# Attention outputs normalised on chip before they are stored: a fused Fourier-mixing and multi-query-attention kernel

## The chip, the cores and the metric

The kernel runs on one core of one Trainium2 chip. The metric is device time in microseconds (us), lower is better. Three runs of the kernel before gave 1739.33, 1739.38 and 1740.87 us, a median of 1739.38 us. Engines are named as the profile names them: PE is TensorE (PEld its weight loads), DVE is VectorE, ACT is ScalarE, POOL is GpSimd, SP is SyncE, which here only issues DMAs.

## The reference

```python
def _A_ref(x, dft_seq_re, dft_seq_im, dft_hid_re, dft_hid_im):
    a = jnp.einsum("bsd,ed->bse", x, dft_hid_re)
    b = jnp.einsum("bsd,ed->bse", x, dft_hid_im)
    return jnp.einsum("ts,bse->bte", dft_seq_re, a) - jnp.einsum("ts,bse->bte", dft_seq_im, b)

def _B_ref(x, wq, wk, wv, wo):          # B, S, D = 1, 2048, 640; H = 32 heads of Dh = 20
    q = (x @ wq).reshape(B, S, H, Dh).transpose(0, 2, 1, 3)
    k = x @ wk                          # one key head and one value head for all
    v = x @ wv
    p = _softmax(jnp.einsum("bhqd,bkd->bhqk", q, k) * (Dh ** -0.5), axis=-1)
    o = jnp.einsum("bhqk,bkd->bhqd", p, v)
    return o.transpose(0, 2, 1, 3).reshape(B, S, H * Dh) @ wo

g = _sigmoid((x * gate_w).sum(-1, keepdims=True))
out = g * _A_ref(x, ...) + (1 - g) * _B_ref(x, ...)
```

All arrays are float32. The change concerns the division by the softmax's sums, between `p @ v` and `@ wo`.

## The kernel before

**Stages.** The first 220 us or so compute queries, keys, values, the gate and the hidden-dimension transform. Then, up to about 1560 us, one long hand-ordered stage interleaves four streams on PE, by a string `PLAN` with one letter per step: `a` matmuls (scores whose row maximum is taken), `b` matmuls (the same scores transposed, from which the probabilities come), `av` matmuls (probabilities times values) and `y` matmuls (the sequence transform). Scores of `a` are reduced by DVE (`mx<-a`, line 363), scores of `b` are exponentiated by ACT (`pt<-b`, line 831). Both kinds share six PSUM banks, so a score matmul waits until DVE or ACT has emptied the bank that it is to write. From about 1560 to 1663 us the last pair's `b` and `av` work runs beside the last `y` products in a loop of 16 rounds (lines 1035 to 1052). Then comes the output projection: 32 groups (`o_group`) of 15 matmuls.

**Heads go in 16 pairs**, each in two halves of 1024 queries (qh = 0, 1). A half's attention output and its softmax sums come out of one PSUM bank, 32 rows for each of two heads times two blocks of 512 queries: 20 rows of output and, in row 20, the sum. `finish_half` (line 847) copies the bank to an SBUF tile `ob` (two buffers, so that a half takes the buffer of the same half of the pair before).

**Sums.** For pairs 0 to 14, once both halves are done, the sums are read back from DRAM as 128 x 32 (`sm`), inverted by DVE 24 ticks later (`finish_sums`), stored (`rec_d`) and spread, by a DMA from DRAM to DRAM, over the 20 rows of each head (`rx_d`). The last pair does the same for each half by itself, 4 ticks later. The projection loads 256 columns of outputs and 256 columns of spread reciprocals (`load_o`), POOL multiplies them (`mult_o`, line 628), DVE splits the product into a high and a low part (`split_o`, lines 644 and 645) and PE multiplies these by the weights.

**What sets the order.** PE, ACT, DVE and POOL execute in the order in which the program is written; `later(n, f)` puts f into it n ticks later, and `tick()` is called once for every two score matmuls. SP's order is not written by hand: the scheduler of the programming layer sets it from the dependences, and SP then issues its DMAs strictly in that order, each after its own waits. `move` (line 118) issues all of them, so line 118 is the line of every DMA. SP goes round eight completion semaphores, and a DMA waits for the one issued eight before it where the program does not yet know that to be done.

Of the kernel before, what the change touches and what calls it, by code (L numbers as in the profile page):

```python
# [8 lines left out]
F32 = mybir.dt.float32  # L9
F32R = mybir.dt.float32r  # L10
AF = mybir.ActivationFunctionType
ALU = mybir.AluOpType
# [5 lines left out]
P = 128  # L18
S = 2048
D = 640  # L20
H = 32
DH = 20
KC = D // P
NT = S // P
NPAIR = H // 2
LAST = NPAIR - 1
# [3 lines left out]
ROW = 512  # L30
# [4 lines left out]
def kernel(  # L35
# [13 lines left out]
    nc = tc.nc  # L49
    ctx.enter_context(tc.manual_schedule(engines={ET.PE, ET.Activation, ET.DVE, ET.Pool}))  # L50

    dram = ctx.enter_context(tc.tile_pool(name="dram", bufs=1, space=DRAM))
# [28 lines left out]
    oT_d = dram.tile([D, S], F32, name="oT_d")  # L81
    m_d = dram.tile([NPAIR, P, 2, 32], F32, name="m_d")
    sum_d = dram.tile([H, S], F32, name="sum_d")
    rec_d = dram.tile([H, S], F32, name="rec_d")
    rx_d = dram.tile([D, S], F32, name="rx_d")
    y_d = dram.tile([S, D], F32, name="y_d")


# [25 lines left out]
    def words(ap):  # L114
        return ap.bitcast(F32) if ap.dtype == F32R else ap

    def move(dst, src, queue=nc.sync):
        queue.dma_start(words(dst), words(src))
# [210 lines left out]
    abp = ctx.enter_context(tc.tile_pool(name="abp", bufs=1))  # L329
# [62 lines left out]
    def later(n, f, *args):  # L392
        todo.append((clock["n"] + n, f, args))

    def tick():
        clock["n"] += 1
        due = [t for t in todo if t[0] <= clock["n"]]
        todo[:] = [t for t in todo if t[0] > clock["n"]]
        for _, f, args in due:
            f(*args)  # L400
# [138 lines left out]
    for t in range(NT):  # L539
# [4 lines left out]
        for i in range(2):  # L544
# [4 lines left out]
            for e in range(2):  # L549
                ps = [rot(f"ab_{t}_{i}_{e}_{g}")[:, :HALF] for g in range(2)]  # L550
                es = slice(e * HALF, (e + 1) * HALF)
                for c in range(KC):
                    mm3_rows(ps, xh[:, c], xl[:, c], wh[i][:, c, es], wl[i][:, c, es], KC, c)
                    n = KC * (4 * (t - 2) + 2 * i + e) + c + 1
# [29 lines left out]
    op = ctx.enter_context(tc.tile_pool(name="op", bufs=2))  # L584


    TW = 2 * P
    wos, oraw, ospl, yrow = {}, {}, {}, {}
# [18 lines left out]
            wos[c] = split_w  # L607

    oT_v = oT_d.rearrange("(c p) t -> p c t", p=P)
    rx_v = rx_d.rearrange("(c p) t -> p c t", p=P)  # L610
    NO = S // TW

    def load_o(n):

        if n < NO:
            oraw[n] = []
            for k, v in enumerate((oT_v, rx_v)):
                if (n % 2, k) == (1, 1):
                    t = op.tile([P, KC, TW], F32, name="oraw", bufs=1)
                else:  # L620
                    t = abp.tile([P, KC, TW], F32, tag=f"ab{5 + 2 * (n % 2) + k}0", name="oraw")
                move(t, v[:, :, n * TW : (n + 1) * TW])
                oraw[n].append(t)

    def mult_o(n):
        if n < NO:
            o, r = oraw[n]
            nc.gpsimd.tensor_tensor(o, o, r, op=ALU.mult)  # L628

    def split_o(n):  # L630
        if n < NO:
            if n % 4 == 0:

                h, l = [
                    qbuf[(LAST + 1 + k) % 3][:, : KC * TW].rearrange("p (c t) -> p c t", c=KC)
                    for k in range(2)
                ]
            else:
                h, l = [
                    abp.tile([P, KC, TW], F32R, tag=f"ab{2 * (n % 4 - 1) + k}1", name="osp")  # L640
                    for k in range(2)
                ]
            o = oraw.pop(n)[0]
            nc.vector.tensor_copy(h, o)
            nc.vector.tensor_tensor(l, o, h.bitcast(F32), op=ALU.subtract)
            ospl[n] = (h, l)

    def load_y(tb):
        if tb < NT:
            yrow[tb] = spare(tb, "yrow")  # L650
            move(yrow[tb], y_d[tb * P : (tb + 1) * P])

    def gate_y(tb):
        if tb < NT:
            nc.scalar.activation(yrow[tb], yrow[tb], AF.Copy, scale=gate[:, tb : tb + 1])
# [3 lines left out]
    def o_group(tb, e):  # L659
        n, k = divmod(tb, 2)  # L660
        es, tk = slice(e * HALF, (e + 1) * HALF), slice(k * P, (k + 1) * P)
        rows = slice(tb * P, (tb + 1) * P)
        ps = orot(f"o_{tb}_{e}")[:, :HALF]
        h, l = ospl[n]
        for c in range(KC):
            mm3(ps, h[:, c, tk], l[:, c, tk], wos[c][0][:, es], wos[c][1][:, es], KC, c)
        oy = op.tile([P, HALF], F32, tag=("yt", "yu")[e], name="oy")
        nc.vector.scalar_tensor_tensor(
            oy, ps, omg[:, tb : tb + 1], yrow[tb][:, es], op0=ALU.mult, op1=ALU.add
        )  # L670
        move(out[rows, es], oy)
# [165 lines left out]
    def av_step(p, qh, kc):  # L837
        if kc == 0:
            av[qh] = bank("V", f"av_{p}_{qh}")
        for hh in range(2):  # L840
            for j in range(2):
                t, slot = pt.pop((hh, kc, 2 * qh + j))
                known["PE"] = max(known["PE"], slot[0])
                av_mm(av[qh], 2 * hh + j, t, kc, kc == 0, kc == NT - 1)
                ptfree.append(slot)

    def finish_half(p, qh):
        ob = op.tile([P, ROW], F32, name="ob")
        nc.scalar.activation(ob, av[qh], AF.Copy)
        for hh in range(2):  # L850
            h = 2 * p + hh
            for j in range(2):
                js = slice((2 * qh + j) * ROW, (2 * qh + j + 1) * ROW)
                g = 32 * (2 * hh + j)
                move(sum_d[h : h + 1, js], ob[g + DH : g + DH + 1])
                move(oT_d[h * DH : (h + 1) * DH, js], ob[g : g + DH])
        if p == LAST:
            sm = op.tile([P, 16], F32, name="sm")
            ts = slice(qh * S // 2, (qh + 1) * S // 2)
            for hh in range(2):  # L860
                move(sm[64 * hh : 64 * hh + 64], sum_d[2 * p + hh, ts].rearrange("(s t) -> s t", t=16))
            later(4, finish_last, ts, sm)
        elif qh == 1:
            sm = op.tile([P, 32], F32, name="sm")
            move(sm, sum_d[2 * p : 2 * p + 2].rearrange("h (s t) -> (h s) t", t=32))
            later(24, finish_sums, p, sm)

    def finish_sums(p, sm):
        rc = op.tile([P, 32], F32, name="rc")
        nc.vector.reciprocal(rc, sm)  # L870
        move(rec_d[2 * p : 2 * p + 2].rearrange("h (s t) -> (h s) t", t=32), rc)
        for hh in range(2):
            h = 2 * p + hh
            move(
                rx_d[h * DH : (h + 1) * DH], rec_d[h : h + 1].to_broadcast([DH, S])
            )

    def finish_last(ts, sm):

        rc = op.tile([P, 16], F32, name="rc")  # L880
        nc.vector.reciprocal(rc, sm)
        for hh in range(2):
            h = 2 * LAST + hh
            move(rec_d[h, ts].rearrange("(s t) -> s t", t=16), rc[64 * hh : 64 * hh + 64])
            move(rx_d[h * DH : (h + 1) * DH, ts], rec_d[h : h + 1, ts].to_broadcast([DH, S // 2]))

    SCORES = "abcdefABCDEFghijklGHIJKL"
    PLAN = (
# [94 lines left out]
    BEFORE = {  # L988
        **{kk: (lambda c=kk - 1: load_wo((c,)),) for kk in range(1, 1 + KC)},
        12: (lambda: load_o(0), lambda: load_o(1)),  # L990
        13: (lambda: mult_o(0), lambda: mult_o(1)),
        14: (lambda: split_o(0), lambda: load_o(2)),
        15: (lambda: [load_y(tb) for tb in range(4)],),
    }
# [10 lines left out]
    def next_v():  # L1005
        st = taken["V"] - LAG
        taken["V"] += 1
        if st >= 0:
            av_step(*STEPS[st])
            if STEPS[st][2] == NT - 1:  # L1010
                finish_half(*STEPS[st][:2])

    for what in PLAN:
# [7 lines left out]
        else:  # L1021
            kind, s = divmod(SCORES.index(what), 6)
# [31 lines left out]
    for _ in range(2):  # L1054
        y_evict()
    split_o(1)
    load_o(3)


    gate_y(0)  # L1060
    for i in range(2 * NT):
        tb, e = divmod(i, 2)
        if e == 0:
            gate_y(tb + 1)
        o_group(tb, e)
        tick()
        if i == 0:
            for st in old:
                av_step(*st)
            finish_half(*old[-1][:2])  # L1070
        n, k = divmod(i, 4)
        if k == 1:
            mult_o(n + 2)
        elif k == 2:
            split_o(n + 2)
            load_o(n + 3 if n else NO)
        if e == 1:
            load_y(tb + 4)
# [47 lines left out]
```

## Time and profile before

| | |
|---|---|
| median of three runs | 1739.38 us |
| the profiled execution | 1738.29 us |
| its span (first to last instruction) | 1736.5 us |
| PE busy | 1725.9 us (99%) |
| DVE busy | 1433.4 us (83%) |
| ACT busy | 1195.2 us (69%) |
| POOL busy | 817.0 us (47%) |
| TensorE clock granted | 1.0 |

A row of the timeline reads: start in us from the span's start, duration in us, engine and line, operation, out<-in, shapes, how many instructions were merged, and in brackets the idle time of that engine just before, with what ended it. SPq rows are DMA issues: what they show is the time that SP spends on the issue, not the transfer. A row of a group reads: busy us and mean ns of one, then the idle time of the engine in front of such instructions and what ended most of it.

### The profile page before, as it was taken

To read this page: it belongs to the slowest core of one execution; us is meant where nothing else is said; L and a number is where in the kernel's file an instruction comes from. 1 tells how busy PE (TensorE), PEld (TensorE's weight loads), DVE (VectorE), ACT (ScalarE), POOL (GpSimd) and SP (SyncE) were. 2 spreads that over 40 slices of the span, in tenths; PEclk is the share of its full clock that TensorE was granted. 3 is DMA by queue.
4 is the path that set the end of the run, shared out by engine and by line. 5 is a ranking of instruction groups with operands and counts; after the bars stand their busy time and mean duration, and the time that the engine had idled before them with its cause. 6 is when DMAs were issued, how large, how long until landed. Compare 5 with 4: busy or idle time off the path is not lost.

```text
span 1736.5 us, 40769 instructions
## 1 busy us (share of the span) xinstructions
PE 1725.9 (99%) x16342; PEld 1214.6 (70%) x16342; DVE 1433.4 (83%) x2355; ACT 1195.2 (69%) x2337; POOL 817.0 (47%) x559
## 2 busy tenths in 40 slices
PE   9999999999999999999999999999999999999998
PEld 8899976666666666666666666666666666667788
DVE  5779998989888898888898889888888898855254
ACT  4722257777777777777777777777777777777731
POOL 1012153563645463756656565565654344542242
PEclk9999999999999999999999999999999999999999
DMA  8873433333344443435453444343443242325667
GB/s 289 242 210 99 129 117 100 121 125 101 121 136 131 117 134 104 155 115 163 133 160 115 156 141 129 110 148 106 142 142 115 85 121 90 95 89 177 200 206 250
DMA packets 131002, 243.88 MB, mean 140 GB/s; under 512 B 26356, under 2 KB 77556, under 8 KB 128292
## 3 DMA queue, kind: packets, MB, share of 16 engines
q1 hardware_dynamic: 130012, 238.00, 43.5%
q0 software_dynamic: 800, 3.28, 0.6%
q8 instruction: 128, 2.10, 0.5%
q14 instruction: 62, 0.51, 0.1%
HBM read 194.62 MB, written 50.86 MB: 141 GB/s over the span
## 4 chain that ended last, share of the span: by engine, by line
PE 90%; DMA 3%; issue 3%; POOL 2%; DVE 2%; SPq 0%; ACT 0%; POOLq 0%; DVEq 0%
PE av L835 26%; PE y L694 19%; PE a L356 17%; PE b L821 16%; PE ab L137 7%; PE q L126 1%; PE q L128 1%; PE q L127 1%; DMA oraw<-rx_d 1%; POOL ya L750 1%; POOL oraw L628 1%; DVE mx L363 0%; DMA wraw<-in_wiT_dram 0%; DMA out_dram<-oy 0%; DMA x_d<-both 0%
## 5 line engine op out<-in xcount | busy, mean ns | idle before, releaser
L363 DVE TENSOR_REDUCE mx<-a 128x1 f32<-128x512 f32 x2048 | 1260.1, 681 | 154.9 <-PE a L356 97.3
L831 ACT ACTIVATE pt<-b 128x512 f32<-128x512 f32 x2048 | 1049.5, 619 | 315.0 <-PE b L821 190.6
L694 PE MATMUL y<-x,ch 64*128 64x320 f32 x3584 | 728.3, 304 | 1.1 <-ACT yt L723 1.1
L356 PE MATMUL a<-ks,qs 60*128 60x512 f32 x2048 | 722.0, 414 | 0.3 <-DVE mx L363 0.2
L821 PE MATMUL b<-qs,ks 62*128 62x512 f32 x2048 | 695.0, 414 | 0.3 <-ACT half L566 0.3
L694 PEld LDWEIGHTS y<-x,ch 64*128 64x128 f32 x3584 | 549.9, 186 | 21.6 <-issue 10.5
L694 PE MATMUL y<-x,cl 64*128 64x320 f32 x1792 | 507.6, 304 | 0.0
L835 PE MATMUL av<-pt,vsb 128*32 128x512 f32 x4096 | 502.9, 600 | 0.0
L356 PEld LDWEIGHTS a<-ks,qs 60*128 60x128 f32 x2048 | 350.5, 184 | 139.9 <-DVE mx L363 102.1
L821 PEld LDWEIGHTS b<-qs,ks 62*128 62x128 f32 x2048 | 340.2, 184 | 139.9 <-ACT pt L831 71.0
L694 PEld LDWEIGHTS y<-x,cl 64*128 64x128 f32 x1792 | 309.8, 185 | 3.4 <-issue 2.5
L482 POOL TENSOR_TENSOR craw<-craw 128x1024 f32<-128x1024 f32 x80 | 189.5, 2369 | 254.6 <-DMA craw<-in_cre_dram 117.5
L835 PEld LDWEIGHTS av<-pt,vsb 128*32 128x32 f32 x4096 | 106.2, 108 | 194.3 <-issue 173.5
L493 POOL TENSOR_TENSOR cl<-craw,ch 128x1024 fp32r<-128x1024 f32 x98 | 232.2, 2369 | 7.9
L492 POOL CAST ch<-craw 128x1024 fp32r<-128x1024 f32 x98 | 101.7, 1037 | 149.1 <-PE y L694 120.1
L137 PE MATMUL ab<-wh,xh 64*128 64x320 f32 x640 | 126.6, 297 | 2.3 <-DVE both L567 1.5
L137 PE MATMUL ab<-wl,xh 64*128 64x320 f32 x640 | 126.2, 296 | 0.0
L137 PE MATMUL ab<-wh,xl 64*128 64x320 f32 x640 | 126.1, 296 | 0.0
L750 POOL TENSOR_TENSOR ya<-yt,ya 128x320 f32<-128x320 f32 x64 | 60.7, 965 | 99.3 <-ACT yt L723 98.7
L566 ACT ACTIVATE half<-ab 128x320 f32<-128x320 f32 x64 | 28.0, 437 | 103.9 <-PE ab L137 98.3
L137 PEld LDWEIGHTS ab<-wh,xl 64*128 64x128 f32 x640 | 92.9, 185 | 0.0
L137 PEld LDWEIGHTS ab<-wl,xh 64*128 64x128 f32 x640 | 92.9, 186 | 0.0
(88 smaller groups left out, 1087.6 us busy)
## 6 DMA issues: line engine op xcount, KB each, us to landing
craw<-in_cre_dram SPq DMA_DIRECT2D x96, 512.0 KB
craw<-in_cim_dram SPq DMA_DIRECT2D x96, 512.0 KB
xr<-x_d SPq DMA_DIRECT2D x88, 320.0 KB
qs<-qh_d SPq DMA_DIRECT2D x64, 160.0 KB
x_d<-both SPq DMA_DIRECT2D x64, 160.0 KB
ya<-y_d SPq DMA_DIRECT2D x64, 160.0 KB
y_d<-ya SPq DMA_DIRECT2D x64, 160.0 KB
xr<-in_xT_dram SPq DMA_DIRECT2D x20, 256.0 KB
```

What stands on the lines that cost most here:

```text
L137: nc.tensor.matmul(ps, w[r], woven(x[r]), start=(i == 0 and k == 0), stop=(i == n - 1 and k == 2))
L356: nc.tensor.matmul(ps, qs[p][b : b + 60, qb * P : (qb + 1) * P], woven(ks[b : b + 60, c * ROW : (c + 1) * ROW]), start=True, stop=True,)
L363: return nc.vector.tensor_reduce(mx[p][:, hh, qb, c : c + 1], ps, axis=AX.X, op=ALU.max)
L482: eng.tensor_tensor(raws[0], raws[0], raws.pop(1), op=PRODUCTS[GROUPS[g][0]][0][1])
L492: eng.tensor_copy(h, raw)
L493: eng.tensor_tensor(l, raw, h.bitcast(F32), op=ALU.subtract)
L566: nc.scalar.activation(half, ps[0], AF.Copy, scale=sg)
L694: mm = nc.tensor.matmul(ps[g % len(ps)], w, woven(x), start=start, stop=stop)
L750: nc.gpsimd.tensor_tensor(ya, yt, ya, op=how)
L821: nc.tensor.matmul(ps, ks[b : b + 62, kc * P : (kc + 1) * P], woven(qs[p][b : b + 62, qc * ROW : (qc + 1) * ROW]), start=True, stop=True,)
L831: halves.scored(nc.scalar.activation(t, ps, AF.Exp, scale=SCALE), n)
L835: nc.tensor.matmul(ps[32 * g : 32 * g + 32, :], vsb[:, kc, :], t, start=first, stop=last)
```

## The change

Outputs are no longer stored raw. `finish_half` stores only the sums. For pairs 0 to 14 the sums are read back and inverted 8 ticks later (24 before); the reciprocals are then loaded from DRAM in spread form, each over 32 rows, into two tiles `rb` (eight DMAs of 32 x 512), and 6 ticks after that POOL multiplies the two `ob` tiles by them (two products of 128 x 512) and eight DMAs store the normalised outputs. For each half of the last pair the raw sums are spread by four DMAs into an `rb` tile, and 4 ticks later DVE inverts the whole 128 x 512 tile, multiplies, and four DMAs store. `rx_d`, the loads from it and the eight POOL products of 128 x 1280 in the projection are gone, and a load of outputs has three buffers.

```diff
-    rx_d = dram.tile([D, S], F32, name="rx_d")
...
         if n < NO:
-            oraw[n] = []
-            for k, v in enumerate((oT_v, rx_v)):
-                if (n % 2, k) == (1, 1):
-                    t = op.tile([P, KC, TW], F32, name="oraw", bufs=1)
-                else:
-                    t = abp.tile([P, KC, TW], F32, tag=f"ab{5 + 2 * (n % 2) + k}0", name="oraw")
-                move(t, v[:, :, n * TW : (n + 1) * TW])
-                oraw[n].append(t)
-
-    def mult_o(n):
-        if n < NO:
-            o, r = oraw[n]
-            nc.gpsimd.tensor_tensor(o, o, r, op=ALU.mult)
+            oraw[n] = abp.tile([P, KC, TW], F32, tag=f"ab{5 + n % 3}0", name="oraw")
+            move(oraw[n], oT_v[:, :, n * TW : (n + 1) * TW])
...
+    obs = {}
+
     def finish_half(p, qh):
-        ob = op.tile([P, ROW], F32, name="ob")
+        ob = obs[p, qh] = op.tile([P, ROW], F32, name="ob")
         nc.scalar.activation(ob, av[qh], AF.Copy)
-        for hh in range(2):
-            h = 2 * p + hh
-            for j in range(2):
-                js = slice((2 * qh + j) * ROW, (2 * qh + j + 1) * ROW)
-                g = 32 * (2 * hh + j)
-                move(sum_d[h : h + 1, js], ob[g + DH : g + DH + 1])
-                move(oT_d[h * DH : (h + 1) * DH, js], ob[g : g + DH])
+        for g, h, js in quarters(p, qh):
+            move(sum_d[h : h + 1, js], ob[g + DH : g + DH + 1])
         if p == LAST:
-            sm = op.tile([P, 16], F32, name="sm")
-            ts = slice(qh * S // 2, (qh + 1) * S // 2)
-            for hh in range(2):
-                move(sm[64 * hh : 64 * hh + 64], sum_d[2 * p + hh, ts].rearrange("(s t) -> s t", t=16))
-            later(4, finish_last, ts, sm)
+            rb = spread(sum_d, p, qh)
+            later(4, finish_last, p, qh, rb)
         elif qh == 1:
             sm = op.tile([P, 32], F32, name="sm")
             move(sm, sum_d[2 * p : 2 * p + 2].rearrange("h (s t) -> (h s) t", t=32))
-            later(24, finish_sums, p, sm)
+            later(8, finish_sums, p, sm)
+
+    def quarters(p, qh):
+        for k in range(4):
+            hh, j = divmod(k, 2)
+            yield 32 * k, 2 * p + hh, slice((2 * qh + j) * ROW, (2 * qh + j + 1) * ROW)
+
+    def spread(src, p, qh):
+        rb = op.tile([P, ROW], F32, name="rb")
+        for g, h, js in quarters(p, qh):
+            move(rb[g : g + 32], src[h : h + 1, js].to_broadcast([32, ROW]))
+        return rb
 
     def finish_sums(p, sm):
         rc = op.tile([P, 32], F32, name="rc")
         nc.vector.reciprocal(rc, sm)
         move(rec_d[2 * p : 2 * p + 2].rearrange("h (s t) -> (h s) t", t=32), rc)
-        for hh in range(2):
-            h = 2 * p + hh
-            move(
-                rx_d[h * DH : (h + 1) * DH], rec_d[h : h + 1].to_broadcast([DH, S])
-            )
...
+        rbs = [spread(rec_d, p, qh) for qh in range(2)]
+        later(6, finish_pair, p, rbs)
+
+    def store_o(p, qh):
+        ob = obs.pop((p, qh))
+        for g, h, js in quarters(p, qh):
+            move(oT_d[h * DH : (h + 1) * DH, js], ob[g : g + DH])
+
+    def finish_pair(p, rbs):
+        for qh in range(2):
+            ob = obs[p, qh]
+            nc.gpsimd.tensor_tensor(ob, ob, rbs[qh], op=ALU.mult)
+            store_o(p, qh)
+
+    def finish_last(p, qh, rb):
+        ob = obs[p, qh]
+        nc.vector.reciprocal(rb, rb)
+        nc.vector.tensor_tensor(ob, ob, rb, op=ALU.mult)
+        store_o(p, qh)
...
-        13: (lambda: mult_o(0), lambda: mult_o(1)),
...
-        if k == 1:
-            mult_o(n + 2)
-        elif k == 2:
+        if k == 2:
```

The change moves instructions on two engines at places of which the prediction speaks. On DVE, the inversion of pair 6's sums (pairs count from 0) stands among the maxima of the `a` scores; the first number in a name `a_...` is the score's number. Before:

```order
L363 TENSOR_REDUCE mx_13871<-a_554_1_14842 128x1
L363 TENSOR_REDUCE mx_13871<-a_555_1_14847 128x1
L870 RECIPROCAL rc_14851<-sm_14326 128x32
L363 TENSOR_REDUCE mx_13871<-a_556_1_14856 128x1
L363 TENSOR_REDUCE mx_13871<-a_552_0_14882 128x1
```

and with the change:

```order
L362 TENSOR_REDUCE mx_13926<-a_536_0_14519 128x1
L362 TENSOR_REDUCE mx_13926<-a_537_0_14529 128x1
L862 RECIPROCAL rc_14559<-sm_14377 128x32
L362 TENSOR_REDUCE mx_13926<-a_538_0_14572 128x1
L362 TENSOR_REDUCE mx_13926<-a_538_1_14575 128x1
```

The inversion now stands in front of 32 maxima that stood in front of it.

On SP, the same pair's DMAs from the sums to the reciprocals. Before:

```order
L118 DMA oT_d<-ob 20x512
L118 DMA y_d<-ya 128x320 x2
L118 DMA sm<-sum_d 128x32
L118 DMA ya<-y_d 128x320 x2
L118 DMA craw<-in_cre_dram 128x1024 x2
L118 DMA xr<-x_d_67 128x640
L118 DMA xr<-x_d_68 128x640
```

and with the change:

```order
L117 DMA sum_d<-ob 1x512 x4
L117 DMA y_d<-ya 128x320 x2
L117 DMA ya<-y_d 128x320 x2
L117 DMA sm<-sum_d 128x32
L117 DMA craw<-in_cre_dram 128x1024 x2
L117 DMA rec_d<-rc 128x32
L117 DMA xr<-x_d_67 128x640
L117 DMA xr<-x_d_68 128x640
L117 DMA rb<-rec_d 32x512 x8
L117 DMA oT_d<-ob 20x512 x8
L117 DMA craw<-in_cre_dram 128x1024 x2
```

The load `sm` of the sums still stands behind the two stores of `ya` (a `y` product's update, made by POOL), and now behind two loads `ya` as well; the inversion's store, the spread loads and the outputs' stores stand ahead of the next `craw` loads.

On DVE in the last rounds, where the last pair's first half is inverted between the splits of the transform's blocks (`ch`, `cl`). Before:

```order
L493 TENSOR_TENSOR cl<-craw,ch 128x1024
L881 RECIPROCAL rc<-sm 128x16
L492 CAST ch<-craw 128x1024
L493 TENSOR_TENSOR cl<-craw,ch 128x1024
```

and with the change:

```order
L492 TENSOR_TENSOR cl<-craw,ch 128x1024
L880 RECIPROCAL rb<-rb 128x512
L881 TENSOR_TENSOR ob<-ob,rb 128x512
L491 CAST ch<-craw 128x1024
L492 TENSOR_TENSOR cl<-craw,ch 128x1024
```

The place is the same; a tile of 512 columns is inverted there instead of 16, and a product follows it.

More of the change, by code (lines that the diff above doesn't have):

```diff
@@ L609 @@
     oT_v = oT_d.rearrange("(c p) t -> p c t", p=P)
-    rx_v = rx_d.rearrange("(c p) t -> p c t", p=P)
     NO = S // TW
@@ L642, in split_o @@
                 ]
-            o = oraw.pop(n)[0]
+            o = oraw.pop(n)
             nc.vector.tensor_copy(h, o)
@@ L871, in finish_sums @@
         move(rec_d[2 * p : 2 * p + 2].rearrange("h (s t) -> (h s) t", t=32), rc)
-        for hh in range(2):
-            h = 2 * p + hh
-            move(
-                rx_d[h * DH : (h + 1) * DH], rec_d[h : h + 1].to_broadcast([DH, S])
-            )
[L878 to L885, printed above, removed]
+        rbs = [spread(rec_d, p, qh) for qh in range(2)]
[14 more added lines that the diff above has]
+        store_o(p, qh)
     SCORES = "abcdefABCDEFghijklGHIJKL"
```

## The prediction

> **What bounds the kernel now.** I read the page's first part, then what PE waited for, then the groups of DVE and PE's weight loads.
>
> ```profile
> span 1736.5 us, 40769 instructions
> PE 1725.9 (99%) x16342; PEld 1214.6 (70%) x16342; DVE 1433.4 (83%) x2355; ACT 1195.2 (69%) x2337; POOL 817.0 (47%) x559
> PE o L128 <- DVE osp L645: 0.9, 1, 0.9
> PE o L128 <- DVE qs L645: 0.7, 1, 0.7
> L363 DVE TENSOR_REDUCE mx<-a 128x1 f32<-128x512 f32 x2048 | 1260.1, 681 | 154.9 <-PE a L356 97.3
> L356 PEld LDWEIGHTS a<-ks,qs 60*128 60x128 f32 x2048 | 350.5, 184 | 139.9 <-DVE mx L363 102.1
> ```
>
> PE is idle for 10.6 us in all (1736.5 - 1725.9), so nothing that leaves PE's work as it is can win more than that. Of these the change can reach two waits, 0.9 and 0.7 us, both in the projection, both for a split output. On the other side PE has little cover: DVE's maxima are 1260.1 us of work, and the weight loads of the `a` scores sat 102.1 us behind a maximum that had yet to empty a bank. So in the long stage DVE must not stand still: what it loses there, PE loses soon after.
>
> **The projection: what is removed.** For the last half the reciprocals go through SP and DRAM three times (`rec_d`, `rx_d`, `oraw`) before POOL can multiply. The rows are the timeline's; the last one is of the stretches, for the tile `o` alone (PE's busy time and its matmuls come first):
>
> ```profile
> 1679.31 1.11 SPq L118 DMA_DIRECT2D rec_d<-rc  x2
> 1686.89 1.10 SPq L118 DMA_DIRECT2D oraw<-rx_d  x1
> 1694.01 2.91 POOL L628 TENSOR_TENSOR oraw<-oraw 128x1280 f32<-128x1280 f32 x1 [19.14 <-DMA oraw<-rx_d]
> 1696.95 0.83 DVE L644 CAST qs<-oraw 128x1280 fp32r<-128x1280 f32 x1 [7.42 <-POOL oraw L628]
> 1699.36 0.40 PE L128 MATMUL o<-wo,qs 128*128 128x320 f32 x1 [0.68 <-DVE qs L645]
> 1664.00:1736.50 72.50, 65.76 (x479) 64.79 (x477) 16.25 (x32) 1.00 0.72 231
> ```
>
> PE stands 0.68 us until the split's low part is there at 1699.3; it wanted it at 1698.7. The second wait, two windows of 256 columns later, has the same form (POOL's product, then the split) and 0.9 us. With the change the way is: sums stored, spread, inverted, multiplied, outputs stored, loaded, split. What is new in it is DVE's work, priced by these groups:
>
> ```profile
> L870 DVE RECIPROCAL rc<-sm 128x32 f32<-128x32 f32 x15 | 5.1, 341 | 0.0
> L881 DVE RECIPROCAL rc<-sm 128x16 f32<-128x16 f32 x2 | 0.5, 253 | 10.6 <-DMA sm<-sum_d 10.6
> L520 POOL TENSOR_TENSOR xr<-xr 128x640 f32<-128x640 f32 x40 | 62.2, 1556 | 0.0
> ```
>
> 16 columns more cost the inversion 88 ns, 5.5 ns each, so 512 columns cost 0.25 + 496 x 0.0055 = 2.98 us (should the slope not hold, not below a product's time); the product half of the 1.23 that a subtraction of 1024 columns takes (row 1629.84 below), with overhead 0.7; together 3.7. The inversion before stood just ahead of the `rec_d` row, near 1678. From there: 3.7, four stores issued and landed 3.3 (issues of 0.25, row 863.77, and 2.2 for a landing, row 1628.50, both below), a load of outputs 7.1 (1686.89 to 1694.01 is one, with issue), the cast 0.83 and the subtraction 1.5: 1694.4. So the first wait goes, with 4 us to spare, and the later windows, which no longer load a second tile nor pass POOL, lose theirs: **-1.7 us** with the restarts (bounds: 0, and 2). DVE's 3.7 us hold up outputs behind them, but an output group of 15 matmuls takes PE 15 x 65.76 / 479 = 2.1 us and seven banks take turns.
>
> **The long stage: the inversion that moves.** Pairs 0 to 14 invert 8 ticks after their second half instead of 24. Pair 6:
>
> ```profile
> 861.33 0.62 ACT L849 ACTIVATE ob<-av 128x512 f32<-128x512 f32 x1
> 863.77 0.25 SPq L118 DMA_DIRECT2D sum_d<-ob  x1
> 871.64 1.70 POOL L750 TENSOR_TENSOR ya<-yt,ya 128x320 f32<-128x320 f32 x2 [3.96 <-ACT yt L723]
> 871.92 7.99 DVE L363 TENSOR_REDUCE mx<-a 128x1 f32<-128x512 f32 x13 [0.41 <-PE a L356]
> 872.53 1.17 SPq L118 DMA_DIRECT2D y_d<-ya  x2
> 873.81 0.37 SPq L118 DMA_DIRECT2D sm<-sum_d  x1
> 874.23 0.92 SPq L118 DMA_DIRECT2D ya<-y_d  x2
> 893.15 0.34 DVE L870 RECIPROCAL rc<-sm 128x32 f32<-128x32 f32 x1
> ```
>
> 24 ticks took 893.15 - 861.33 = 31.8 us, so 8 take 10.6 and the inversion's new place is at 871.9, just where the run of 13 maxima starts (the order: 32 places earlier, at about 0.6 us each). But SP, which issues in its order, had stored the sums by 864 and then stood behind `y_d<-ya` until POOL gave the `ya` at 872.5; only then came `sm`, at 873.81. In the new order two `ya` loads stand ahead of `sm` too: 872.53 + 1.17 + 0.92 + some gaps = 874.7. How long such a load takes to land, the last pair's first half shows:
>
> ```profile
> 1626.31 0.50 SPq L118 DMA_DIRECT2D sm<-sum_d  x1
> 1628.50 0.25 DVE L881 RECIPROCAL rc<-sm 128x16 f32<-128x16 f32 x1 [10.57 <-DMA sm<-sum_d]
> 1629.84 1.23 DVE L493 TENSOR_TENSOR cl<-craw,ch 128x1024 fp32r<-128x1024 f32 x1
> 1633.29 0.30 PE L694 MATMUL y<-x,ch 64*128 64x320 f32 x2
> ```
>
> 2.2 us, with DVE waiting for nothing else. So pair 6's sums are in SBUF at 876.9 and DVE stands still from 871.9: **5.0 us**. Behind the inversion on DVE stand the 13 maxima, and PE waits for their banks. It has an `av` run and a spare bank or two in hand, which I put at 0.5 us, since the 13 maxima are back to back and the delay passes to the last of them. PE loses **4.5 us** (bounds 3.5 and 5). That cannot be made up: the matmuls behind are the same and PE was never idle there.
>
> Pair 4 is the second such place, for another reason: two 512 KB `craw` loads are issued just ahead of the sums' stores, and these come down behind them.
>
> ```profile
> 684.60 0.60 ACT L849 ACTIVATE ob<-av 128x512 f32<-128x512 f32 x1 [0.24 <-PE av L835]
> 689.49 0.42 SPq L118 DMA_DIRECT2D craw<-in_cim_dram  x1
> 690.80 0.21 SPq L118 DMA_DIRECT2D sum_d<-ob  x1
> 695.10 0.21 SPq L118 DMA_DIRECT2D sum_d<-ob  x1
> 697.29 0.35 SPq L118 DMA_DIRECT2D sm<-sum_d  x1
> 717.95 0.34 DVE L870 RECIPROCAL rc<-sm 128x32 f32<-128x32 f32 x1
> ```
>
> A third of 717.95 - 684.60 is 11.1: the new place is 695.7. The four stores of sums no longer alternate with the outputs' stores, so the last is issued near 692 instead of 695.1; `sm` follows when they have landed. If nothing were in their way, `sm` at 694 and no wait; if the loads hold them as before, `sm` at 697.3, in SBUF at 699.5, and a wait of 3.8. The loads are the same, so I take the middle, 1.9, less 0.2 of cover: **1.7 us**. Pair 9 has two such loads ahead of it and its reckoning ends even:
>
> ```profile
> 1130.39 0.60 ACT L849 ACTIVATE ob<-av 128x512 f32<-128x512 f32 x1
> 1141.46 0.34 SPq L118 DMA_DIRECT2D sm<-sum_d  x1
> ```
>
> (new place near 1141.5, and `sm` not much earlier than 1141). For it and its like (in pairs 5, 7 and 8 too a large load or a wait for POOL stands just ahead of `sm`) I take **0.5 us** together; bounds 0, and 2 each. In the other pairs the new place leaves more room.
>
> **The long stage: what is added.** Per pair two POOL products of 128 x 512, 1556 x 512/640 = 1.25 us each, 37 us in all; and on SP 26 DMAs in place of 20, with `craw` loads behind outputs' stores that wait for POOL. Both are covered by POOL's lead:
>
> ```profile
> L482 POOL TENSOR_TENSOR craw<-craw 128x1024 f32<-128x1024 f32 x80 | 189.5, 2369 | 254.6 <-DMA craw<-in_cre_dram 117.5
> L492 POOL CAST ch<-craw 128x1024 fp32r<-128x1024 f32 x98 | 101.7, 1037 | 149.1 <-PE y L694 120.1
> ```
>
> POOL waited 120.1 us for PE to give a `ch` buffer back, which only an engine that is ahead does. Such a lead is half a group of `y` matmuls or more, over 10 us by the count of steps, and a pair's late loads take up to 10 of it and have 80 us to give it back. I cost this at nothing; without the lead each late microsecond of a `cl` would be one of PE's. ACT's next copy into an `ob` comes half a pair, some 45 us, after the inversion, and finds the outputs stored.
>
> **The last rounds.** At 1628.50 DVE waits for the first half's sums; behind stands a split whose `cl` ended at 1629.84 + 1.23 = 1631.1, wanted by PE at 1633.3 by count of the steps (the last row). 3.7 instead of 0.25 us would end it at 1634.5, 1.2 late; but the spread loads follow the sums' stores at once and come about 1.5 earlier than the second `sm` did. I take **0.3 us** (bounds 0 and 1.5).
>
> **Sum:** -1.7 + 4.5 + 1.7 + 0.5 + 0.3 = +5.3. The profiled execution took 1738.29 us, its span 1736.5 and 1.8 around it; with the change span 1741.8 and 1743.6. The median before is 1.1 above the profiled execution: **1744.7 us**.
>
> **Rivals.**
> (1) *The sums come in time.* `sm` lands before DVE reaches the inversion, or DVE's idle share (154.9 us before the maxima) swallows the wait. For it: four DMAs fewer stand ahead of `sm`. Against it: in pair 6 SP stands behind POOL, whatever its list. Then the projection's gain is left, 1739.4 - 1.7 = 1737.7; with half of pair 6's wait, 1739.9. 0.25.
> (2) *SP becomes the brake* (slower). SP stands at the outputs' stores until POOL has multiplied, `craw` is late by more than POOL's lead, and PE waits at the next `cl`. It decides from a delay of about 12 us in a pair; at 5 us in one pair of three it adds 25 to the waits above: some 1765; in one or two pairs, 1752. For it: `rb` and stores are 16 DMAs in a row. Against it: the 120.1 us. 0.11.
> (3) *POOL's products hold DVE up* (slower). Here these rows:
>
> ```profile
> 861.91 4.87 DVE L363 TENSOR_REDUCE mx<-a 128x1 f32<-128x512 f32 x8 [0.18 <-PE a L356]
> 867.24 4.28 DVE L363 TENSOR_REDUCE mx<-a 128x1 f32<-128x512 f32 x7 [0.45 <-PE y L694]
> 1657.95 3.52 DVE L644 CAST qs<-oraw 128x1280 fp32r<-128x1280 f32 x1 [3.64 <-POOL oraw L628]
> ```
>
> The cast took 3.52 us at 1657.95, beside a POOL product, and 0.83 at 1696.95, alone. If 30 products held a maximum each for their 1.25 us, 37 us: 1777. Against it: 8 maxima took 0.609 us each while POOL worked, 7 took 0.611 while it mostly waited. 0.01. [...]
> (4) *More goes than the two waits*, by a traffic without `rx_d` that feeds the long stage earlier: PE waits for no DMA there, so little can be won; 1734. 0.03.
>
> **How the numbers follow.** The forecast has 0.60, and by the bounds of its terms its own range is 1741 to 1748. A difference of 0.2% (3.5 us, about what a measurement of this kernel can tell) puts 1742.9 as the edge of slower: 0.51 of the 0.60 lies above it, with (2) and (3) 0.63. Of (1) 0.21 is within, with 0.09 of the forecast 0.30. Faster is below 1735.9: the rest of (1) and (4), 0.07. The range that leaves out 2 in 10 reaches down into (1), 1738, and up past the forecast's own, 1750.
>
> **What would show it.** Right: DVE's inversions (group `rc<-sm`) with idle time ahead of them ended by the DMA `sm<-sum_d`, near 5 us in one and 2 to 3 in another, and PE idle on maxima in the long stage, where it has none now; no wait of `o` for `osp` or `qs`; an inversion of 512 columns near 3 us. Wrong: no idle time ahead of `rc` (then rival 1), or PE waiting at `y` for `cl` (rival 2), or maxima longer than 681 ns (rival 3).

## The result, and the profile after

The changed kernel takes **1762.47 us** (median of 4 runs, 1757.29 to 1764.73) where the kernel before, run beside it, takes 1739.39: a ratio of 1.0126, 95% interval 1.0102 to 1.0151. Forecast were 1744.7 and a range of 1738 to 1750. The direction was right, the size was not: 23 us slower, not 5.

Of the changed kernel, the span, the busy times and three groups of DVE:

```profile
span 1762.4 us, 40890 instructions
...
PE 1737.7 (99%) x16342; PEld 1222.9 (69%) x16342; DVE 1436.6 (82%) x2357; ACT 1196.4 (68%) x2337; POOL 829.1 (47%) x581
...
L362 DVE TENSOR_REDUCE mx<-a 128x1 f32<-128x512 f32 x2048 | 1260.7, 681 | 158.6 <-PE a L355 98.8
...
L880 DVE RECIPROCAL rb<-rb 128x512 f32<-128x512 f32 x2 | 6.7, 3346 | 9.5 <-DMA rb<-sum_d 9.5
L862 DVE RECIPROCAL rc<-sm 128x32 f32<-128x32 f32 x15 | 5.2, 346 | 14.3 <-DMA sm<-sum_d 14.3
```

Two things differ. PE is idle for 24.7 us (1762.4 - 1737.7) where it was for 10.6. And the same 16342 matmuls now keep it busy for 11.8 us more. The maxima take 681 ns as before, so POOL's products do not hold DVE up. The inversions `rc<-sm` now have 14.3 us of DVE's idle time ahead of them, ended by the load of the sums; before they had none. What PE waited for (us in total, times, longest):

```profile
PE a L355 <- DVE mx L362: 8.0, 4, 4.2
PE b L808 <- DVE mx L362: 3.2, 2, 2.7
PE ab L136 <- DVE both L566: 2.7, 1, 2.7
...
PE b L808 <- DMA qs<-m_d: 1.0, 1, 1.0
PE y L681 <- DVE cl L492: 0.7, 1, 0.7
```

The waits of `o` for `osp` and `qs` are gone, as forecast; 11.2 us of waits for maxima have come, in the long stage, where there were 0.2. The timeline at pair 6, on SP:

```profile
872.22 1.11 SPq L117 DMA_DIRECT2D sum_d<-ob  x4
882.78 1.17 SPq L117 DMA_DIRECT2D y_d<-ya  x2
884.00 0.92 SPq L117 DMA_DIRECT2D ya<-y_d  x2
885.08 0.32 SPq L117 DMA_DIRECT2D sm<-sum_d  x1
```

on DVE:

```profile
877.48 4.27 DVE L362 TENSOR_REDUCE mx<-a 128x1 f32<-128x512 f32 x7 [0.47 <-PE y L681]
887.82 0.35 DVE L862 RECIPROCAL rc<-sm 128x32 f32<-128x32 f32 x1 [6.06 <-DMA sm<-sum_d]
```

and on PE:

```profile
884.12 0.48 PE L808 MATMUL b<-qs,ks 62*128 62x512 f32 x1
888.77 0.79 PE L355 MATMUL a<-ks,qs 60*128 60x512 f32 x1 [4.16 <-DVE mx L362]
```

The stores of the sums are issued by 873.3, SP then stands until POOL has given `ya` at 882.8, `sm` follows at 885.1, DVE stands 6.06 us and PE 4.16. But PE's first matmul behind the stop takes 0.79 us, where an `a` takes 0.41 on the mean. The stretches around it show why (a row has, after the length: busy time of PE, PEld, DVE, ACT and POOL with their instructions, the granted clock, the DMA share, GB/s):

```profile
881.30:884.70 3.40, 3.31 (x27) 1.14 (x23) 0.45 (x1) 1.65 (x5) 1.70 (x2) 1.00 0.20 73
884.70:888.13 3.43, 0.00 (x0) 0.00 (x0) 0.32 (x2) 0.54 (x1) 0.00 (x0) 1.00 0.77 237
888.13:891.54 3.41, 2.77 (x15) 2.68 (x17) 3.41 (x7) 1.20 (x2) 0.64 (x1) 0.50 0.99 354
891.54:894.96 3.42, 3.42 (x24) 3.42 (x23) 2.67 (x5) 2.28 (x4) 3.27 (x3) 0.50 0.70 163
894.96:898.40 3.44, 3.44 (x34) 1.66 (x34) 2.97 (x6) 2.64 (x5) 3.44 (x3) 1.00 0.10 31
```

From 888.13 to 894.96 the granted clock is 0.50: two stretches of 3.41 us, in each of which a busy PE gets through 1.7 us less work (an estimate, 0.50 x 3.41). In all traces of this case the lowest clock is 0.50, and by the clock's records it stays there for 3.413 us (in the first profile of the changed kernel at 103.06, 1164.61 and 1591.27) or twice that (6.827 at 888.13; longer at one place of experiment 4, where PE stood for 13.6 us; what follows the last matmul is left out). A stop here therefore cost its length and then 0, 1.7 or 3.4 us.

Where the time came from, by the delay of ACT's instructions against the same instructions in the first trace of the kernel before (the median over 20 us, read behind each place), for the first profile of the changed kernel and for a second one taken later (experiment 6):

| place | forecast | first profile | second profile |
|---|---|---|---|
| first 100 us, untouched by the change | none | +5.4 | +0.3 |
| pair 4 | +1.7 | +2.9 | +4.9 |
| pair 6 | +4.5 | +7.1 | +6.0 |
| pairs 5, 7, 8 and 9 | +0.5 | +7.0 | +5.0 |
| a load of `qs` that SP issues late (near 860) | none | +1.4 | +1.2 |
| the rest of the long stage | none | +0.4 | +0.7 |
| half clock behind PE's 1.1 us wait for `yt`, a wait that was there before too | none | +1.7 | +1.7 |
| last rounds | +0.3 | +1.6 | +1.4 |
| projection | -1.7 | -1.6 | -1.5 |
| sum (differences of the spans: 25.9 and 19.6) | +5.3 | +25.9 | +19.7 |

Without the first row, which is not the change's doing (experiment 7), the two profiles are 20.5 and 19.4 us late.

### The profile page after: what moved, and what is told of

Its sections match the earlier page's. It is cut to its first block, busy times and chain, and to the rows that moved or that the text cites. A ratio compares the mean times of both kernels' runs of the same rounds, so it can differ in the third digit from the quotient of the medians.

```text
span 1762.4 us, 40890 instructions
## 1 busy us (share of the span) xinstructions
PE 1737.7 (99%) x16342; PEld 1222.9 (69%) x16342; DVE 1436.6 (82%) x2357; ACT 1196.4 (68%) x2337; POOL 829.1 (47%) x581
## 4 chain that ended last, share of the span: by engine, by line
PE 88%; DMA 4%; POOL 4%; DVE 1%; issue 1%; SPq 1%; ACT 1%; POOLq 0%; DVEq 0%
PE av L822 25%; PE y L681 19%; PE b L808 15%; PE a L355 15%; PE ab L136 7%; PE o L125 1%; PE o L126 1%; PE o L127 1%; PE q L125 1%; PE q L126 1%; DMA craw<-in_cim_dram 1%; PE q L127 1%; POOL cl L492 1%; POOL craw L481 1%; DMA sm<-sum_d 1%; DVE mx L362 1%
```

## The experiments

Theory W (waits and clock): DVE's waits for the sums stop PE, and the stops bring stretches at half clock. Theory T (traffic): the products on POOL, the added DMAs and SP's order cost the time.

**1. 14 ticks.**

```
-            later(8, finish_sums, p, sm)
+            later(14, finish_sums, p, sm)
```

> The changed kernel with one number altered: the inversion of pairs 0 to 14 is called 14 ticks after the half instead of 8 (18.6 us instead of 10.6). Theory W (waits and clock): the changed kernel loses its time where DVE stands at an inversion whose sums are not yet loaded, PE stops behind it, and the granted clock falls for some us after the longer stops. Against the trace of before, ACT's copies are later by 2.9 us behind pair 4, 0.7 behind pair 5, 7.1 behind pair 6, 1.3, 0.9 and 4.2 behind pairs 7, 8 and 9: 17.1 in all. The latest sums of the changed kernel's trace (pair 6) are loaded 15.6 us after the half's copy, so with 18.6 no inversion waits, and all of the 17.1 go: 1762.5 - 17.1 = 1745.4. What is left above the kernel before is then 5.4 us of delay in the first 100 us, of which W says nothing, and some 2 us of a late load of qs and of the last rounds, less the two waits of the projection. Theory T (traffic): the products on POOL, the six added DMAs per pair and SP's new order cost the time, and the inversion is only where it shows; then 14 ticks move little, and the time stays above 1757.

Measured: 1741.61 us (11 runs, 1740.42 to 1745.03) beside 1739.16 for the kernel before (20 runs, 1736.52 to 1742.94), ratio 1.0016 (1.0007 to 1.0025). From its groups:

```profile
L362 DVE TENSOR_REDUCE mx<-a 128x1 f32<-128x512 f32 x2048 | 1260.4, 681 | 155.5 <-PE a L355 97.7 <-PE b L808 48.1 <-PE y L681 7.8
...
L355 PE MATMUL a<-ks,qs 60*128 60x512 f32 x2048 | 722.6, 414 | 0.4 <-DVE mx L362 0.2
...
L862 DVE RECIPROCAL rc<-sm 128x32 f32<-128x32 f32 x15 | 5.1, 341 | 0.0
```

No inversion waits, PE's idle time ahead of `a` is 0.4 us, and 21 of the 23 us are gone, with all products, DMAs and the new projection kept. T is refuted. The time is 4 us under what W said; W had left the 5.4 us of the first 100 us in its sum (experiment 7 is on these).

**2. The same places without the wait.**

```
-            later(8, finish_sums, p, sm)
+            later(8, finish_sums, p, old_sm.get("sm", sm))
+            old_sm["sm"] = sm
```

> The changed kernel, 8 ticks as it is, but the inversion of pair p reads the loaded sums of pair p-1, which have been in SBUF for 80 us (pair 0 reads its own). All loads and stores, POOL's products and the places of all instructions stay; what is changed in the computation is that the outputs of pairs 1 to 14 are divided by the sums of another pair. W: the inversion never waits, PE is idle for it nowhere, and the 17.1 us of the long stage go: about 1745.4, as with 14 ticks. T: nothing of the traffic is changed, so the time stays above 1757. If the two kernels (this one and the one with 14 ticks) differ by more than 3 us, the place of the inversion costs something else than its wait.

Measured: 1742.37 us (9 runs), ratio 1.0021 (1.0010 to 1.0032), 0.8 us from experiment 1. Its waits of PE, the first lines:

```profile
PE ab L136 <- DVE both L566: 1.4, 1, 1.4
PE warm L267 <- POOL ident masks.py:199: 1.4, 1, 1.4
PE b L808 <- DMA qs<-m_d: 1.3, 1, 1.3
```

So the place 8 ticks after the half costs nothing by itself; the wait there does. What is left of the traffic is the third line: with 8 ticks SP reaches a load of `qs` too late, 1.3 us here and 1.0 in the changed kernel. In experiment 1, with 14 ticks, that wait isn't there (experiment 5, also with 14, has one of 0.4 us at another place).

**3. The moved inversion alone, in the kernel before.**

```
-            later(24, finish_sums, p, sm)
+            later(8, finish_sums, p, sm)
```

> The kernel before with one number altered: the inversion is called 8 ticks after the half instead of 24. No product on POOL, no added DMA; the outputs still go through rx_d. W: in the trace of before the loads of the sums are issued at 697.3, 873.8, 1141.5 and 1320.5 (pairs 4, 6, 9, 11) and land some 2.1 us later; the new places of the inversions are 695.6, 871.9, 1141.9 and 1315.2. DVE stands 3.8, 4.0, 1.7 and 7.4 us, PE some 0.8 less each: 13.7; the clock falls after three of these for 1.5 to 3 us of lost time each: about 7. 1739.4 + 21 = 1760, with waits of PE for mx in the long stage. T: no added traffic, so 1739 to 1741.

Measured: 1756.93 us (4 runs), ratio 1.0095 (1.0078 to 1.0112). Its waits of PE:

```profile
PE a L356 <- DVE mx L363: 6.0, 3, 3.6
PE b L821 <- DVE mx L363: 4.9, 2, 3.8
```

One number moves the kernel before by 17.8 us, without a product or a DMA more. PE stops for 3.6 us at pair 4, 1.1 at pair 5, 2.3 at pair 6 and 3.8 at pair 9. Pair 11 does not wait: in the new order its `sm` is issued 4.0 us behind the half, where it was 13.8. W had counted a wait of 7.4 us there.

**4. Doses.** In the kernel before, 8 ticks after each pair's second half:

```
+            later(8, hold_dve, p)
...
+    dz = op.tile([P, ROW], F32, name="dz", bufs=1)
+    nc.vector.memset(dz, 1.0)
+    def hold_dve(p):
+        for n in ((256,), (384,), (512,), (512, 128), (512, 256))[p % 5]:
+            nc.vector.reciprocal(dz[:, :n], dz[:, :n])
```

> The kernel before, with DVE held up on purpose 8 ticks after each pair's second half by inversions of a scratch tile that nothing else reads or writes: 256, 384, 512, 512 + 128 and 512 + 256 columns in turn over the pairs, about 1.75, 2.55, 3.35, 4.3 and 5.1 us by the 3.35 us that 512 columns took in the changed kernel; three pairs for each. It adds 3 x 17.05 = 51 us of DVE work and no DMA. W: PE stops some 0.8 us shorter than DVE is held (39 us in all), and after stops of about 2.6 us or more the granted clock falls, which adds 1.5 to 3 us each on 6 to 9 of the pairs: 1739.4 + 39 + 20 = 1798, and the delay behind a pair is larger than PE's stop there. A rival of W's second half (the clock in the records is only a mark, and stops cost no more than their length): 1778, and the delay behind each pair equals PE's stop.

Measured: 1811.86 us (2 runs). 14.8 us of it were not meant: DVE stood 13.2 us ahead of the scratch tile's fill at 251.6 (that its memory came free only then is the author's reading; the trace names nothing that ended the wait). Without that some 1797. The scratch tile's groups:

```profile
L874 DVE RECIPROCAL dz<-dz 128x512 f32<-128x512 f32 x9 | 30.1, 3342 | 0.0
L874 DVE RECIPROCAL dz<-dz 128x256 f32<-128x256 f32 x6 | 10.5, 1747 | 0.1
L874 DVE RECIPROCAL dz<-dz 128x384 f32<-128x384 f32 x3 | 7.6, 2543 | 0.0
L874 DVE RECIPROCAL dz<-dz 128x128 f32<-128x128 f32 x3 | 2.9, 953 | 0.1
```

PE's longest single stop behind each dose, the delay behind the pair (as in the table above), and how many stretches of 3.41 us at clock 0.50 lie between:

| DVE held | stops, us | delay, us | stretches at 0.50 |
|---|---|---|---|
| 1.75 | 1.0, under 0.3, 0.5 | 1.2, 1.0, 0.6 | 0, 0, 0 |
| 2.5 | 1.2, under 0.3, 1.4 | 1.6, 1.8, 3.8 | 0, 0, 1 |
| 3.3 | 2.5, 3.0, 2.8 | 4.7, 4.5, 4.4 | 1, 1, 1 |
| 4.3 | 3.8, 3.5, 3.9 | 5.7, 6.5, 6.5 | 1, 2, 2 |
| 5.1 | 4.5, 4.9, (pair 14: none) | 6.3, 7.3, 0 | 1, 2, 0 |

Two stretches of it, behind one of the 3.3 us doses and behind one of the 5.1:

```profile
542.55:545.97 3.42, 3.42 (x17) 0.88 (x17) 3.08 (x6) 0.60 (x1) 0.74 (x1) 0.50 0.41 147
...
1201.40:1204.70 3.30, 3.30 (x20) 0.89 (x14) 0.57 (x1) 0.00 (x0) 0.00 (x0) 0.50 0.62 199
```

From a stop of 1 us on, the delay is the stop and then some 1.7 us for each stretch at half clock (behind small ones the delay is up to 1.8 us where the matmuls' modelled ends leave hardly a stop to be seen): the rival, stops that cost their length alone, is out. DVE hides only a little of a delay, and from a hold of 3.3 us on every stop of PE brought at least one stretch.

**5. 14 ticks, and the last pair's first half later.**

```
-            later(4, finish_last, p, qh, rb)
+            later(8 - 4 * qh, finish_last, p, qh, rb)
```

> The kernel with 14 ticks, and besides the inversion of the last pair's first half called 8 ticks after that half instead of 4, so that on DVE one more split of the transform stands ahead of it, and not behind its wait of 8.24 us for the spread sums. In the trace of the kernel with 14 ticks the last rounds are 1.4 us later than before (PE's 0.6 us wait for cl and a lower clock behind it), the long stage 0.4 us, the projection 2.0 us quicker, and the first 100 us 3.2 us slower, although the order of work is the same there. W: the 1.4 us go, 1741.6 - 1.4 = 1740.2, if the 3.2 us at the start belong to the kernel; 1739.2 + 0.4 - 2.0 = 1737.6, if they are chance that any kernel of this case meets. Theory T (traffic) has no place left where it would cost more than 0.5 us.

Measured: 1743.21 us (11 runs), ratio 1.0020 (1.0011 to 1.0029): a miss, no quicker than experiment 1. PE still waits for `cl`, 1.0 us where it was 0.6 in experiment 1. What delays the block is not the one split.

**6. The changed kernel again.** No edit.

> The changed kernel once more, for a second profile. W: DVE waits for the sums at the same pairs (4 to 9), PE's stops there are within 0.5 us of the first profile's (2.6, 4.2 and 2.7 us at pairs 4, 6 and 9), but what the lower clock adds behind each varies between 0 and 3 us, since it did so behind stops of equal length in the trace with doses; time 1757 to 1765. If the clock's part were fixed for each place, the delays behind the pairs would be those of the first profile (2.9, 7.1 and 4.2 us).

Measured: 1757.86 and 1765.71 us. Stops of 3.0, 4.2 and 2.3 us at pairs 4, 6 and 9 (2.6, 4.2 and 2.7 in the first profile), delays of 4.9, 6.0 and 2.4 (2.9, 7.1 and 4.2). The stops are the kernel's, the clock behind them is not fixed. Pair 4 in this profile:

```profile
697.60:701.10 3.50, 0.58 (x5) 0.43 (x5) 1.53 (x4) 0.68 (x2) 3.36 (x3) 1.00 0.39 101
701.10:704.50 3.40, 3.40 (x20) 0.88 (x18) 2.35 (x4) 0.60 (x1) 3.26 (x4) 0.50 0.63 205
```

and in the first one, where PE's stop of 2.61 us falls into two such stretches and no half clock follows:

```profile
700.40:703.81 3.41, 1.96 (x21) 1.65 (x17) 0.81 (x2) 2.70 (x6) 3.27 (x3) 1.00 0.25 55
703.81:707.22 3.41, 2.25 (x19) 1.11 (x23) 3.20 (x6) 0.60 (x1) 3.41 (x2) 1.00 0.48 105
```

**7. The kernel before again.** No edit.

> The kernel before once more, for a second profile. The profiles so far of six kernels with the same order of work in the first 100 us differ there by 0 to 5.4 us, the kernel before being the quickest. If that is chance, this profile may be 1 to 4 us later there too, with a longer stop of PE at ab (1.5 us in the first profile) and, from about 2 us on, a lower clock behind it. If it belongs to the kernels, this one is within 0.3 us of the first profile.

Measured: 1741.82 us (8 runs, 1737.40 to 1745.34). This profile is 4.2 us late after the first 100 us: a stop of 2.1 us at `ab`, and behind it:

```profile
99.30:102.70 3.40, 1.27 (x17) 1.03 (x17) 0.89 (x2) 0.44 (x1) 0.00 (x0) 1.00 0.87 238
102.70:106.20 3.50, 3.50 (x32) 3.50 (x30) 0.49 (x1) 0.44 (x1) 0.00 (x0) 0.51 0.82 237
```

In the eleven profiles of this case the first 100 us cost 0 to 5.4 us, with the same order of work. So the 5.4 us of the changed kernel's first profile are chance, not the change. This profile also shows a wait of 0.7 us for `cl` in the last rounds, where the first had none.

**8 and 9. What makes the last rounds late.** Experiment 8 keeps 14 ticks and the last pair's first half at 8, and calls loads of outputs later:

```
-        12: (lambda: load_o(0), lambda: load_o(1)),
-        14: (lambda: split_o(0), lambda: load_o(2)),
-        15: (lambda: [load_y(tb) for tb in range(4)],),
+        12: (lambda: load_o(0),),
+        14: (lambda: split_o(0), lambda: load_o(1)),
+        15: (lambda: [load_y(tb) for tb in range(4)], lambda: load_o(2)),
```

> The kernel with 14 ticks and the last pair's first half at 8 ticks, and besides the projection's second and third load of outputs (640 KB each) called two rounds and one round later (14 and 15 of the last rounds in place of 12 and 14), so that the second-to-last load of the transform's blocks is no longer issued behind two of them. In the trace with the loads as they were, DVE waited 14.65 us for that block and PE 1.0 us for its cl, 1.2 us with the clock behind it; a second profile of the kernel before has the same wait with 0.7 us, its first has none. W: if the outputs' loads make the block late, the wait for cl goes, and the time is 1.2 us lower than with the loads early, about 1742.0; with the projection's 2.0 us left it is within 2 us of the kernel before on either side. If the block is late for another reason (SP behind the stores of ya), the wait stays at 0.5 to 1.0 us and the time at 1743.

Measured: 1741.20 us (12 runs), ratio 1.0014 (1.0002 to 1.0025). The wait stays, 0.7 us for `cl` and 0.8 ahead of it. Experiment 9 has the inversion 12 ticks after the half, and `load_o(0)` in round 13 (the other loads as in experiment 8):

```
-            later(8 - 4 * qh, finish_last, p, qh, rb)
+            later(12 - 8 * qh, finish_last, p, qh, rb)
```

> The kernel with 14 ticks, and the inversion of the last pair's first half 12 ticks after it instead of 4 (the projection's first three loads of outputs then one, two and one rounds later, as they have to be), so that on DVE two more splits of the transform stand ahead of the inversion. In the trace with 8 ticks DVE stood 5.9 us for the spread sums and 4.0 at the inversion and its product, the two splits behind gave their buffers back at 1639.5 and 1641.4, and the next block's load was issued at 1641.9, right behind. W: the last rounds' wait for cl (1.5 us, 2.0 with what hangs on it) comes from there; with the splits ahead the load is issued some 3 us earlier and the wait is under 0.3 us, and the time 2 us lower than with 8 ticks: 1739.2, as the kernel before. If the wait stays above 0.7 us, it is the transfers of outputs (three of 640 KB ahead of the last block) that make the block late; 1741.

Measured: 1740.60 us (12 runs), ratio 1.0011 (1.0000 to 1.0023). The inversion waits for nothing now, yet PE's wait for `cl` is 1.0 us. SP in experiment 9:

```profile
1630.86 0.42 SPq L117 DMA_DIRECT2D craw<-in_cre_dram  x1
...
1643.61 1.52 SPq L117 DMA_DIRECT2D oraw<-oT_d  x3
1645.55 0.60 SPq L117 DMA_DIRECT2D craw<-in_cre_dram  x1
```

and DVE:

```profile
1634.82 0.69 DVE L491 CAST ch<-craw 128x1024 fp32r<-128x1024 f32 x1 [8.21 <-DMA craw<-in_cre_dram]
...
1641.95 1.89 DVE L492 TENSOR_TENSOR cl<-craw,ch 128x1024 fp32r<-128x1024 f32 x1
1654.93 1.38 DVE L491 CAST ch<-craw 128x1024 fp32r<-128x1024 f32 x1 [11.09 <-DMA craw<-in_cre_dram]
```

The last block is issued right behind three loads of 640 KB, and DVE gets it 9.4 us later. The block issued at 1630.86, with no load of outputs just ahead of it, came 4.0 us after its issue. That fits the second half of the expectation (the outputs' transfers make the block late), but no run took these loads from ahead of the block: in every order tried loads of outputs stood there. It stays a likely cause, not a shown one. Experiments 1, 5, 8 and 9 all end 0.11 to 0.20% above the kernel before, too near to each other to be told apart. None beats it.

## Why the prediction was right or wrong

**The chain of cause: right.** The inversion on DVE waits for `sm<-sum_d`, PE stops behind its maxima, and this outweighs the projection's gain. Experiments 1, 2 and 3 show it from three sides: called later, without the wait, and alone.

**Pair 6: right in the stop.** The forecast had 12.8 us from the end of the half's copy to the issue of `sm`, 5.0 of DVE's standing and 4.5 of PE's. Measured are 12.9 (872.2 to 885.1), 6.06 and 4.16.

**Pair 4: nearer the far bound.** The step took the middle, 1.9, between no wait and 3.8, since four stores fewer alternate. The timeline of the changed kernel on SP:

```profile
696.28 1.10 SPq L117 DMA_DIRECT2D sum_d<-ob  x4
...
702.37 0.34 SPq L117 DMA_DIRECT2D sm<-sum_d  x1
```

and on DVE:

```profile
704.02 0.35 DVE L862 RECIPROCAL rc<-sm 128x32 f32<-128x32 f32 x1 [2.81 <-DMA sm<-sum_d]
```

The stores are issued in one piece, but 5.0 us go by before `sm` can follow them. `sm` goes out 11.6 us after the end of the half's copy, where it was 12.1 before. DVE's wait was 2.8 us here and 3.2 in the second profile, PE's stop 2.6 and 3.0, against 1.7 in the sum.

**Pairs 5, 7, 8 and 9: the step that failed first.** "Its reckoning ends even" set the new place at 1141.5 against the *issue* of `sm` at 1141. The inversion waited for the landing, 2.52 us of DVE's time. The changed kernel on DVE:

```profile
1159.64 1.88 DVE L362 TENSOR_REDUCE mx<-a 128x1 f32<-128x512 f32 x3
1164.03 0.35 DVE L862 RECIPROCAL rc<-sm 128x32 f32<-128x32 f32 x1 [2.52 <-DMA sm<-sum_d]
```

`sm` was issued at 1160.87, the place was reached at 1161.5, both as reckoned; the 2.2 us that the forecast itself had read for a landing were used for pairs 4 and 6 and left out here. Pairs 5, 7 and 8 waited 1.0 us each, for the same reason. The bound "2 each" held for the stops, except at pair 9 (2.7 and 2.3); the value of 0.5 for all together did not.

**The clock: a step that failed, with no term in the sum.** The forecast let PE lose as long as it stands. Behind the first 110 us the two profiles of the changed kernel have 4 and 3 stretches of 3.41 us at clock 0.50. One of them in each follows the wait for `yt`, which was there before too; the other 3 and 2 follow stops behind maxima and are 5.1 and 3.4 us of lost work. The first trace of before has none (its clock is 1.00 from first to last), which is why its rows gave no price. In the traces since, the clock fell to 0.50 behind most stops of 2.1 to 3.0 us (not behind the 2.6 us at pair 4 in the first profile, nor the 2.3 at pair 9 in the second), and behind some of 1.1; behind the stop of 4.16 us at pair 6, for which the forecast had 4.5, it stayed there for 6.83 us.

**POOL's products and six more DMAs at nothing: nearly right.** Experiment 2 has them all, and of its traces only the late `qs` (1.3 us) belongs to them in the long stage. The products take 1278 ns, the forecast had 1250. Rivals 1 and 3 fall, and of rival 2 (SP as the brake) only this remainder is left; its 1765 also left out the 5.3 us of the other terms that it meant to add to, and by its own reckoning was some 1770.

**The last rounds: mis-sized.** The term was 0.3, bounds 0 to 1.5; 1.6 and 1.4 came. The inversion of 512 columns took 3.35 us, not 2.98. The forecast looked at the split behind it; the wait came at a later block. 0.7 us of such a wait can come in the kernel before too (experiment 7).

**The projection: right.** No wait of `o` is left, and -1.6 and -1.5 us stand against the forecast's -1.7.

Put together: PE's stops behind maxima were 11.2 and 12.1 us (of the 12.1, 0.8 came at the place of the late load of `qs`) instead of the 6.7 of the sum, and the half clock that follows these stops, 5.1 and 3.4 us, was left out altogether. The width of the range failed with that: each of its bounds was a bound of a stop's length.

## What to carry to other kernels

In this kernel, whose PE is busy for 99% of the span, most stops of some 2 us or more had a second price: 1.7 us for each stretch at half clock behind them, 0 to 2 of them. So in a kernel like it reckon stops longer than 2 us at up to twice their length (the 2.5 us of experiment 4 came to 4.7, the 4.16 at pair 6 to 7.1). Which of them brought a stretch went with how much of the stop lay in one stretch of 3.413 us (last section). A moved wait is set against the landing of what it waits for, at every place alike, and a place with two possible values near the path takes the later one. Where a result isn't needed soon, leave the consumer late: 6 ticks more, 8 us, took away 21 us here, while the gain that the change was after was under 2 us and lies within what the first 100 us differ by from run to run.

## What the hardware showed that was not expected

The wait of 1.07 us for `yt` near 1567 is in all eleven profiles, at the same place of the work, and 1.07 us long in each. In five of them a stretch at half clock follows and costs 1.7 us, in six none does. With it (experiment 5):

```profile
1565.10:1568.50 3.40, 2.33 (x22) 2.05 (x19) 0.00 (x0) 2.88 (x6) 0.32 (x1) 1.00 0.00 0
1568.50:1572.00 3.50, 3.50 (x26) 3.50 (x26) 0.00 (x0) 2.17 (x4) 1.35 (x2) 0.51 0.45 133
```

and without (experiment 8):

```profile
1565.80:1569.20 3.40, 2.33 (x20) 2.05 (x18) 0.00 (x0) 2.88 (x6) 0.33 (x1) 1.00 0.00 0
1569.20:1572.60 3.40, 3.40 (x47) 3.40 (x47) 0.00 (x0) 3.04 (x7) 1.35 (x2) 1.00 0.47 128
```

Within a run the changes of the clock lie whole multiples of 3.413 us apart (in the first profile of the changed kernel at 103.06, 106.48, 888.13, 894.96, 1164.61, 1168.02, 1591.27 and 1594.69). Carried on at that spacing, a run's own changes cut it into stretches of 3.413 us. Adding up how long PE stands in each (without the first 20 us and the last 5), and counting over the eleven traces, gives:

| PE stands within one stretch | stretches | next stretch at 0.50 | among them: start, PE stands, next clock |
|---|---|---|---|
| at full clock, up to 1.06 us | all others | none | changed kernel 860.82, 1.03, 1.00; before 95.25, 1.02, 1.00 |
| at full clock, 1.07 to 1.81 us | 28 | 8 | changed kernel 1587.86, 1.07, 0.50 and 700.39, 1.45, 1.00 |
| at full clock, 1.83 us and more | 19 | 19 | changed kernel 99.65, 2.69, 0.50; 884.71, 3.41, 0.50; 1161.19, 2.29, 0.50 |
| at 0.50, up to 0.38 us | 27 | none | changed kernel 1164.61, 0.38, 1.00 |
| at 0.50, 0.64 us and more | 7 | 7 | changed kernel 888.13, 0.64, 0.50; experiment 4 1198.00, 1.65, 0.50 |

These are counts of this case's traces; what makes the clock fall they do not show. The two stops of pair 4 differ by how they fall into the stretches: the first profile's 2.61 us lie 1.45 in one and 1.16 in the next, and 2.83 of the second profile's 2.98 us lie in one. Pair 6 had two stretches at 0.50 where PE stood 0.64 us in the first of them (first profile), and one where it stood 0.09 (second). The wait for `yt` lies in the range between. In the five traces with half clock behind it, it begins 1.8 to 2.2 us after the start of a stretch (1.91 in the changed kernel); in the six without, 0.5 to 0.7 us after one (three) or 2.3 us and more (three, with 2.59 in the kernel before). Why its place within the stretch counts is open, and no run moved a stop against the stretches.
